# Windowed attention and an MLP mixer on one core: engine order fixed by hand throughout, token weights over SyncE's queue

## The chip, the cores and the metric

The kernel runs on one core of a Trainium2 chip. The metric is device microseconds (us) of one execution; smaller is better. A core has five engines with queues of their own: TensorE (PE; its weight loads are listed as PEld), VectorE (DVE), ScalarE (ACT), GpSimd (POOL) and SyncE (SP). An engine works through its queue in order and waits at an instruction whose inputs or buffers are not free yet.

## The reference

Inputs are q, k, v of shape (8 batches, 8 heads, 576 positions, 64), token-mixing weights (576 x 256 and 256 x 576) and channel-mixing weights (512 x 1536 and 1536 x 512), all float32. With x the attention output laid out as (batch, 576, 512):

```
scores = q @ k.T / 8, less slope(head) * |distance|; only 0 <= distance < 128 counts
x = softmax(scores) @ v
u = x + (relu(x.T @ w_tok1) @ w_tok2).T          # mixes the 576 positions
out = u + relu(u @ w_ch1) @ w_ch2                # mixes the 512 channels
```

## The kernel before

**Tiling.** 576 positions are four blocks of 128 and a rest of 64. Batches go in pairs: a pair has nine blocks, 0 to 3 of its first batch, 4 to 7 of its second, and block 8 (`TAIL`), which holds both rests. The first batch of a pair (half 0) does attention for blocks 0 to 3 and TAIL, the second (half 1) for 4 to 7. Since the window is 128, a block needs its own keys and those of the block before; blocks 0 and 4 need only their own.

**Attention of a block** (`attention`, lines 266 to 300). q and k come in bfloat16 over POOL's queue (`load`, line 95), which converts them on the way; PE transposes them into one PSUM tile `tp` (line 193; eight transposes, four for q and four for k) and VectorE copies that to `qkT` (line 286; line 429 in the first batch). PE makes the scores (line 215) for the even and the odd heads (e = 0, 1) into two PSUM tiles `sp`, one buffer each; ScalarE takes the exponential (line 228) into `pe`; VectorE multiplies by a mask (line 235, `weigh`) that holds the window and the decay with distance; PE multiplies by v (line 253, `values`) into `ot`, whose 65th column is the sum of weights; VectorE normalises (`normalise`: reciprocal, line 259, and product, line 261) into `xb`. Values of one block are emitted after the scores of the next (`held`).

**Token mixing** (`token_mix`): `t1` (line 316) with a relu on ScalarE (line 318) into r1; then for each block `ht` (line 334), to which VectorE adds x (line 335) to give `ub`, and then, after all of these, four transposes of ub (line 340), copied to `uT` (line 346).

**Channel mixing** (`channel_mix`): 12 tiles `ct` of four 512-column matmuls each (line 360), each with a relu on ScalarE (line 362) into r2; in half 1 also three groups `cx` of 16 matmuls of 128 columns for TAIL (line 369). Then, for each of four blocks (five in half 1), 12 matmuls into `o2` (line 378), an add on VectorE (line 382) and the output DMA on SP's queue (lines 385 and 387).

**PSUM.** `tp`, `ot` and `ut` share the pool ps_o with one buffer; `t1`, `ht`, `ct`, `cx` and `o2` share ps_m with three.

**What sets the order.** POOL's queue has the order of the program for the whole kernel (`manual_schedule`). The first batch's attention and token mixing (`first_batch`) are in a second such block, which also fixes PE, ScalarE and VectorE among its own instructions. All that follows on these three engines is put in order by the framework's scheduler, from a cost model of its own and the order of the program; it may set later work between the first batch's instructions. The program mixes batch b's channel mixing with the attention and token mixing of batch b + 1 (`side`) by estimated costs, the numbers after `yield` in ns: `interleave` advances the side until it has done a share (0.78; 1.2 for batch 0, after a lead of 7000 ns) of what the channel mixing has.

**The start.** POOL issues 20 loads of q, k and v for the first batch, then six of the token weights (lines 158 to 166; W1, W2 and their rests, converted to bfloat16 on the way), then the four quarters of the first channel weights (line 173), then blocks 4 to 6 and the four quarters of the second channel weights (line 177). In `first_batch` VectorE also makes masks for TAIL (`make_tail_mask`, lines 141 to 144) in the first two blocks' iterations, and both q and k copies (`settle`). At the end come ht, accumulated on x with the identity (line 494) and W2 (line 503), casts to ub (line 508, on ScalarE and VectorE in turn), and the transposes and copies to uT (lines 452 and 453, `turn_u`), one block behind.

Of the kernel before, what the change touches and what calls it, by code (L numbers as in the profile page):

```python
# [16 lines left out]
def kernel(  # L17
# [47 lines left out]
    ps_m = ctx.enter_context(tc.tile_pool(name="ps_m", bufs=3, space=PS))  # L65

# [90 lines left out]
    def load_token_weights():  # L157
        nc.gpsimd.dma_start(
            out=W1[:, 0:NC, :], in_=moe_w_tok1[0 : NC * P, :].rearrange("(c p) n -> p c n", p=P)
        )  # L160
        w2 = moe_w_tok2.rearrange("(j p) s -> p j s", p=P)
        for i in range(2):
            nc.gpsimd.dma_start(out=W1[i * R : (i + 1) * R, NC + i, :], in_=moe_w_tok1[NC * P : S, :])
        nc.gpsimd.dma_start(out=W2[:, :, :], in_=w2[:, :, 0 : NC * P])
        for i in range(2):
            nc.gpsimd.dma_start(out=W2t[:, i, :, i * R : (i + 1) * R], in_=w2[:, :, NC * P : S])

# [98 lines left out]
    def attention(b):  # L266
# [38 lines left out]
    def token_mix(b):  # L305
# [6 lines left out]
        for j in range(NJ):  # L312
# [5 lines left out]
            nc.scalar.activation(out=r1[:, j, :], in_=t1[:, :], func=ACT.Relu)  # L318
            yield 1080
        r1s[pr, half] = r1  # L320
        uT = rpool.tile([P, NCB, NC * P], BF16, name="uT", tag="uT")
        uTt = None
        if half:
            blocks.append(TAIL)
            uTt = rpool.tile([P, NCB, P], BF16, name="uTt", tag="uTt")
        for blk in blocks:
            ht = ps_m.tile([P, DM], F32, name="ht", tag="m")
            if blk == TAIL:
                mms = [(W2t[:, i, j, :], r1s[pr, i][:, j, :]) for i in range(2) for j in range(NJ)]
            else:  # L330
                c = blk % NC
                mms = [(W2[:, j, c * P : (c + 1) * P], r1[:, j, :]) for j in range(NJ)]
            for n, (l, r) in enumerate(mms):
                nc.tensor.matmul(ht[:, :], lhsT=l, rhs=r, start=n == 0, stop=n == len(mms) - 1)  # L334
            nc.vector.tensor_tensor(out=us[pr][:, blk, :], in0=ht[:, :], in1=xb[:, blk, :], op=ALU.add)  # L335
            yield 432
        for blk in blocks:
            ut = ps_o.tile([P, NCB, P], BF16, name="ut", tag="o")
            for cb in range(NCB):
                nc.tensor.transpose(ut[:, cb, :], us[pr][:, blk, cb * P : (cb + 1) * P], ident[:, :])  # L340
            if blk == TAIL:
                to = uTt[:, :, :]
            else:
                c = blk % NC
                to = uT[:, :, c * P : (c + 1) * P]
            nc.vector.tensor_copy(out=to, in_=ut[:, :, :])
            yield 225
        uts[b] = (uT, uTt)


    def channel_mix(b):
# [5 lines left out]
        for t in range(NHT):  # L357
# [4 lines left out]
            nc.scalar.activation(out=r2[:, t, :], in_=ct[:, :], func=ACT.Relu)  # L362
            yield 864
            if half and t % 4 == 3:
# [6 lines left out]
                nc.scalar.activation(out=r2t[:, t - 3 : t + 1, :], in_=cx[:, :, :], func=ACT.Relu)  # L371
                yield 900
        blocks = list(range(half * NC, (half + 1) * NC)) + ([TAIL] if half else [])
        for blk in blocks:
            o2 = ps_m.tile([P, DM], F32, name="o2", tag="m")
            for t in range(NHT):
                l = r2t[:, t, :] if blk == TAIL else r2[:, t, (blk % NC) * P : (blk % NC + 1) * P]
                nc.tensor.matmul(o2[:, :], lhsT=l, rhs=WC2[:, t, :], start=t == 0, stop=t == NHT - 1)  # L378
                if t % 3 == 2 and t < NHT - 1:
                    yield 648  # L380
            ob = opool.tile([P, DM], F32, name="ob", tag="ob")
# [4 lines left out]
            else:  # L386
                nc.sync.dma_start(out=out[b, (blk % NC) * P : (blk % NC + 1) * P, :], in_=ob[:, :])
            yield 648

# [15 lines left out]

# [6 lines left out]
    def first_batch():  # L412
# [41 lines left out]

        make_masks()
        turn(0)
        settle(0, "q")
        settle(0, "k")
        held = None
        for n, u in enumerate(units):  # L460
# [3 lines left out]
            pe = [exponentials(u, 0, sp[0])]  # L464
            scores(0, u, sp, (1,))
            for blk in nxt:
                turn(blk)
                settle(blk, "q")
                settle(blk, "k")
            pe.append(exponentials(u, 1, sp[1]))  # L470
            if held is not None:
# [5 lines left out]
            else:  # L477
# [84 lines left out]
```

## Time and profile before

| | us |
|---|---|
| median of 3 runs (334.94 to 336.82) | 335.84 |
| the profiled execution, its own time | 334.79 |
| its span, first to last instruction | 333.0 |

| engine | busy us | share of the span | instructions |
|---|---|---|---|
| PE | 306.8 | 92% | 2692 |
| PEld | 165.1 | 50% | 2692 |
| DVE | 169.9 | 51% | 389 |
| ACT | 136.9 | 41% | 208 |
| POOL | 112.1 | 34% | 143 |

The profile has a page (busy time, slices of the span, DMA queues, the chain of work that ended last, the costliest groups of instructions, DMA issues), and the trace under it can be asked for a timeline, for waits, and for busy time by stage. In a line like `x8 [0.30 <-DVE xb L261]` eight instructions are merged, and the engine was idle 0.30 us before them until VectorE had written xb at line 261. In lines by stage the numbers after the stretch are its length, the busy time of PE, PEld, DVE, ACT and POOL with their counts, the granted PE clock, the DMA share and GB/s. A PE line's duration includes the way out of the array, so the next line can start before it ends.

### The profile page before, as it was taken

The page shows a single profiled execution, that of the slowest core. Times are in us where ns is not written, and L with a number is a line of the kernel's source. Part 1 is how long each engine was busy: PE and PEld are TensorE (multiplying, and loading weights), DVE is VectorE, ACT ScalarE, POOL GpSimd, SP SyncE. Part 2 cuts the span into 40 slices and gives each one's busy share as a digit, 9 for nine tenths or more (in the row PEclk, how much of TensorE's full clock was granted, in tenths as well). Part 3 has the DMA queues.
Part 4 walks back from the last instruction along what each step waited for, and adds up shares of the span by engine and source line. Part 5 has one row for each costly group of instructions (what it writes and reads, how often), then busy time and mean ns, then how long its engine had stood idle before and what let it go on. Part 6 is the DMA issues. An engine that isn't in the chain of part 4 may idle for free.

```text
span 333.0 us, 6446 instructions
## 1 busy us (share of the span) xinstructions
PE 306.8 (92%) x2692; PEld 165.1 (50%) x2692; DVE 169.9 (51%) x389; ACT 136.9 (41%) x208; POOL 112.1 (34%) x143
## 2 busy tenths in 40 slices
PE   1787699689999999999999999999999999999993
PEld 1573345335655555455564555455654555455541
DVE  2594306755665646464656547474756447461021
ACT  4451266312864037503863047404772057404600
POOL 8997777799874020523654000000000000000000
PEclk9999699979999999999999999999999999999999
DMA  8999999999999161594999220011000220011022
GB/s 54 145 135 173 162 197 160 179 126 166 171 105 102 65 113 15 35 137 85 107 85 80 94 65 2 1 63 66 2 2 21 75 63 2 0 65 63 2 78 81
DMA packets 123005, 27.81 MB, mean 84 GB/s; under 512 B 113888, under 2 KB 118368, under 8 KB 122976
## 3 DMA queue, kind: packets, MB, share of 16 engines
q0 software_dynamic: 117728, 17.97, 75.4%
q1 hardware_dynamic: 5248, 9.44, 8.3%
q8 instruction: 21, 0.34, 0.4%
q14 instruction: 8, 0.07, 0.1%
HBM read 35.91 MB, written 9.44 MB: 136 GB/s over the span
## 4 chain that ended last, share of the span: by engine, by line
PE 81%; POOL 5%; DVE 5%; DMA 5%; issue 2%; ACT 1%; POOLq 0%
PE o L378 28%; PE ct L360 24%; PE sp L215 5%; PE tp L193 5%; PE ot L253 5%; PE t L316 5%; PE ht L334 4%; DMA kld<-in_k_dram 3%; PE cx L369 3%; PE ut L340 2%; DMA v<-in_v_dram 2%; DVE pe L235 2%; DVE xb L261 2%; POOL kld L95 2%; POOL qld L95 1%
## 5 line engine op out<-in xcount | busy, mean ns | idle before, releaser
L362 ACT ACTIVATE r<-ct 128x512 bf16<-128x512 f32 x96 | 56.2, 601 | 123.4 <-PE ct L360 123.4
L360 PE MATMUL ct<-uT,WC 128*128 128x512 bf16 x384 | 98.3, 384 | 0.1
L378 PE MATMUL o<-WC,r 128*128 128x512 bf16 x384 | 96.4, 379 | 0.5
L228 ACT ACTIVATE pe<-sp 128x1024 bf16<-128x1024 f32 (+1 forms) x72 | 63.0, 927 | 22.5 <-PE sp L215 22.5
L378 PEld LDWEIGHTS <-r 128*128 128x128 bf16 x384 | 35.7, 98 | 36.8 <-issue 2.5
L360 PEld LDWEIGHTS <-WC 128*128 128x128 bf16 x384 | 34.2, 99 | 30.5 <-issue 2.1
L382 DVE TENSOR_TENSOR ob<-o,ub 128x512 f32<-128x512 f32 x36 | 24.7, 687 | 46.2 <-PE o L378 46.2
L235 DVE TENSOR_TENSOR pe<-pe,mask 128x1024 bf16<-128x1024 bf16 (+1 forms) x64 | 39.0, 618 | 17.9 <-ACT pe L228 17.2
L95 POOL DMA_DIRECT2D qld<-in_q_dram x40 | 34.8, 873 | 33.9 <-PE tp L193 29.9
L95 POOL DMA_DIRECT2D v<-in_v_dram x40 | 34.6, 875 | 27.1 <-PE ot L253 13.9
L95 POOL DMA_DIRECT2D kld<-in_k_dram x40 | 34.6, 869 | 5.0 <-DMA WC<-in_moe_w_ch_dram 2.1
L335 DVE TENSOR_TENSOR ub<-ht,xb 128x512 bf16<-128x512 f32 x32 | 21.4, 687 | 23.5 <-PE ht L334 22.9
L253 PE MATMUL ot<-v,pe 128*128 128x65 bf16 (+1 forms) x544 | 29.6, 199 | 3.5 <-DVE xb L261 3.3
L253 PEld LDWEIGHTS <-pe 128*128 128x128 bf16 (+1 forms) x544 | 22.3, 102 | 21.2 <-DVE xb L261 16.4
L286 DVE COPY qkT<-tp 128x1024 bf16<-128x1024 bf16 (+1 forms) x31 | 21.2, 683 | 21.9 <-PE tp L193 21.9
L261 DVE TENSOR_TENSOR xb<-ot,rt 128x256 bf16<-128x256 f32 x72 | 30.5, 424 | 2.4
L215 PE MATMUL sp<-qkT 64*128 64x128 bf16 (+1 forms) x544 | 25.7, 225 | 3.1 <-DVE qkT L429 3.0
L215 PEld LDWEIGHTS <-qkT 64*128 64x128 bf16 x544 | 18.6, 99 | 16.8 <-DVE qkT L286 11.6
L259 DVE RECIPROCAL rt<-ot 128x4 f32<-128x4 f32 x72 | 12.8, 178 | 24.1 <-PE ot L253 23.7
L193 PE MATMUL tp<-ident,qld 128*128 128x128 bf16 x144 | 15.3, 234 | 8.5 <-DMA qld<-in_q_dram 7.5
L316 PE MATMUL t<-xb,W 128*128 128x512 bf16 x70 | 20.2, 393 | 0.7 <-DVE xb L261 0.7
L193 PEld LDWEIGHTS <-qld 128*128 128x128 bf16 x144 | 10.0, 103 | 17.1 <-DMA qld<-in_q_dram 7.9
(58 smaller groups left out, 198.4 us busy)
## 6 DMA issues: line engine op xcount, KB each, us to landing
out_dram<-ob SPq DMA_DIRECT2D x32, 256.0 KB, 2.0
qld<-in_q_dram POOLq DMA_DIRECT2D x32, 128.0 KB, 5.6
kld<-in_k_dram POOLq DMA_DIRECT2D x32, 128.0 KB, 5.3
v<-in_v_dram POOLq DMA_DIRECT2D x32, 128.0 KB, 6.1
WC<-in_moe_w_ch_dram POOLq DMA_DIRECT2D x8, 384.0 KB, 8.4
out_dram<-ob SPq DMA_DIRECT2D x8, 128.0 KB, 2.3
qld<-in_q_dram POOLq DMA_DIRECT2D x8, 64.0 KB, 5.1
kld<-in_k_dram POOLq DMA_DIRECT2D x8, 64.0 KB, 4.3
```

The source lines that it names most:

```text
L95: nc.gpsimd.dma_start(out=got[x][p0 : p0 + n, :, 0:D], in_=rows(SRC[x], b, s0, n))
L193: nc.tensor.transpose(tp[:, "qk".index(x) * NHP + hp, :], loaded[pr, blk][x][:, 2 * hp : 2 * hp + 2, :].rearrange("p h d -> p (h d)"), ide ...
L215: nc.tensor.matmul(sp[e][:, i, kind, c0:c1], lhsT=qkT[pr, kb][e * D : (e + 1) * D, NHP + i, :], rhs=me[e * D : (e + 1) * D, i, c0:c1], sta ...
L228: nc.scalar.activation(out=pe[:, :, f:, :], in_=sp[:, :, f:, :], func=ACT.Exp, scale=scale)
L235: nc.vector.tensor_tensor(out=pe[:, :, f:, :], in0=pe[:, :, f:, :], in1=mk[:, :, f:, :], op=ALU.mult)
L253: nc.tensor.matmul(ot[to, i, :], lhsT=l, rhs=r, start=m == 0, stop=m == len(mms) - 1, skip_group_check=True)
L261: nc.vector.tensor_tensor(out=x4[:, :, e, :], in0=ot[:, :, 0:D], in1=rt[:, :, :].broadcast_to([P, 4, D]), op=ALU.mult)
L316: nc.tensor.matmul(t1[:, :], lhsT=W1[:, c, j * P : (j + 1) * P], rhs=xb[:, blk, :], start=n == 0, stop=n == len(ks) - 1)
L360: nc.tensor.matmul(ct[:, :], lhsT=WC1[:, cb, t * P : (t + 1) * P], rhs=uT[:, cb, :], start=cb == 0, stop=cb == NCB - 1)
L362: nc.scalar.activation(out=r2[:, t, :], in_=ct[:, :], func=ACT.Relu)
L378: nc.tensor.matmul(o2[:, :], lhsT=l, rhs=WC2[:, t, :], start=t == 0, stop=t == NHT - 1)
L382: nc.vector.tensor_tensor(out=ob[:, :], in0=o2[:, :], in1=ub[:, blk, :], op=ALU.add)
```

## The change

- `attention`, `token_mix` and `channel_mix` move into the block that fixes PE, ScalarE and VectorE, so that these three keep the program's order for the whole kernel.
- `interleave` goes. `alternate` advances the side by one step after a step of channel mixing; a side step says by the number that it yields after how many steps the next one comes (1 or 2; 1 at most in batch 0, where five steps of channel mixing run first).
- In `attention` weighing half 1 moves to the start of the next unit's step, and weighing half 0 behind the normalising of half 1 of the unit before. Values of halves 0 and 1 are separate steps, as before.
- In `token_mix` the transposes of a block's u come with the next block's ht instead of after all of them.
- Token weights come as float32 over SP's queue (four DMAs, issued first) into a staging tile in a buffer of r2, and VectorE rounds them to bfloat16 in two groups of copies, one before the first unit and one within it. Both tail masks are made before the first unit.
- In `first_batch` ScalarE instead of VectorE copies q of every block but the first. The exponential of half 1 of the first unit comes before the copies.
- PE gets matmuls of ones with ones into an unused PSUM tile `idle`, which takes a ps_m buffer: 9 at the start, 2 after the first transposes, 8 after the first scores, 3 at the end of each of four units.

The diff, shortened:

```diff
     ps_m = ctx.enter_context(tc.tile_pool(name="ps_m", bufs=3, space=PS))
+    ones = const.tile([P, DM], BF16, name="ones")
+    nc.vector.memset(ones, 1.0)
...
     def load_token_weights():
+        stage = rpool.tile([P, (NC + 1) * DTOK + NJ * S], F32, name="stage", tag="r2")
+        s1 = stage[:, 0 : (NC + 1) * DTOK].rearrange("p (c n) -> p c n", n=DTOK)
+        s2 = stage[:, (NC + 1) * DTOK :].rearrange("p (j s) -> p j s", s=S)
+        nc.sync.dma_start(
+            out=s1[:, 0:NC, :], in_=moe_w_tok1[0 : NC * P, :].rearrange("(c p) n -> p c n", p=P)
         )
         for i in range(2):
+            nc.sync.dma_start(out=s1[i * R : (i + 1) * R, NC, :], in_=moe_w_tok1[NC * P : S, :])
+        nc.sync.dma_start(out=s2[:, :, :], in_=moe_w_tok2.rearrange("(j p) s -> p j s", p=P))
+        return s1, s2
+
+    def round_token_weights(s1, s2, which):
+        copy = nc.vector.tensor_copy
+        if which == 0:
+            copy(out=W1[:, 0:NC, :], in_=s1[:, 0:NC, :])
+            for i in range(2):
+                rs = slice(i * R, (i + 1) * R)
+                copy(out=W1[rs, NC + i, :], in_=s1[rs, NC, :])
+        else:
+            copy(out=W2[:, :, :], in_=s2[:, :, 0 : NC * P])
+            for i in range(2):
+                copy(out=W2t[:, i, :, i * R : (i + 1) * R], in_=s2[:, :, NC * P : S])
...
     def attention(b):
...
-                yield 450
+                yield 1
             got = None
+            if held is not None:
+                weigh(held[0], 1, held[1][1])
             if u is not None:
                 sp = [score_tile(e) for e in range(2)]
                 scores(pr, u, sp, (0, 1))
                 got = (u, [exponentials(u, e, sp[e]) for e in range(2)])
-                for e in range(2):
-                    weigh(u, e, got[1][e])
-                yield 700
-            if held is not None:
-                for e in range(2):
+            for e in range(2):
+                if held is not None:
                     normalise(pr, held[0], e, values(pr, held[0], e, held[1][e], ps_o, "o"))
-                    yield 300
+                if got is not None and e:
+                    weigh(u, 0, got[1][0])
+                yield 1
             held = got
...
     def token_mix(b):
...
-            yield 1080
+            yield 1 + (j == NJ - 1)
...
-        for blk in blocks:
+        for n, blk in enumerate(blocks + [None]):
...
+            if n:
+                last = blocks[n - 1]
+                ut = ps_o.tile([P, NCB, P], BF16, name="ut", tag="o")
...
+            yield 2
...
-    def interleave(main, other, share, lead):
-        done_m, done_o = -float(lead), 0.0
-        for cost in main:
-            done_m += cost
-            while done_o < done_m * share:
-                c = next(other, None)
-                if c is None:
-                    break
-                done_o += c
+    def alternate(main, other, lead, most):
+        for _ in main:
+            lead -= 1
+            if lead < 0:
+                lead = min(next(other, 1), most) - 1
...
     def first_batch():
...
+        idle = ps_m.tile([P, DM], F32, name="idle", tag="m")
+
+        def keep_busy(n):
+            for _ in range(n):
+                nc.tensor.matmul(idle[:, :], lhsT=ones[:, 0:P], rhs=ones[:, :], start=True, stop=True)
+
+        keep_busy(9)
...
             to = qk_tile(0, blk)
-            nc.vector.tensor_copy(out=to[:, sl, :], in_=tp[:, sl, :])
+            if x == "q" and blk:
+                nc.scalar.copy(out=to[:, sl, :], in_=tp[:, sl, :])
+            else:
+                nc.vector.tensor_copy(out=to[:, sl, :], in_=tp[:, sl, :])
...
         turn(0)
+        keep_busy(2)
         settle(0, "q")
         settle(0, "k")
+        round_token_weights(*staged, 0)
+        for e in range(2):
+            make_tail_mask(e)
...
             scores(0, u, sp, (1,))
+            if n == 0:
+                keep_busy(8)
+                pe.append(exponentials(u, 1, sp[1]))
             for blk in nxt:
                 turn(blk)
                 settle(blk, "q")
                 settle(blk, "k")
-            pe.append(exponentials(u, 1, sp[1]))
+            if n:
+                pe.append(exponentials(u, 1, sp[1]))
...
-                if n < 2:
-                    make_tail_mask(n)
+                if n == 0:
+                    round_token_weights(*staged, 1)
             held = (u, pe)
+            if u != TAIL:
+                keep_busy(3)
...
         with tc.manual_schedule(engines={ET.PE, ET.Activation, ET.DVE}):
+            staged = load_token_weights()
             first_loads()
-            load_token_weights()
...
             first_batch()
-        other = side(1)
-        for b in range(B):
-            interleave(channel_mix(b), other, *((1.2, 7000) if b == 0 else (0.78, 0)))
+            other = side(1)
+            alternate(channel_mix(0), other, 5, 1)
             drain(other)
-            other = side(b + 2)
+            for b in range(1, B):
+                other = side(b + 1)
+                alternate(channel_mix(b), other, 0, 2)
+                drain(other)
```

More of the change, by code (lines that the diff above doesn't have):

```diff
@@ L157, in load_token_weights @@
     def load_token_weights():
-        nc.gpsimd.dma_start(
-            out=W1[:, 0:NC, :], in_=moe_w_tok1[0 : NC * P, :].rearrange("(c p) n -> p c n", p=P)
+        stage = rpool.tile([P, (NC + 1) * DTOK + NJ * S], F32, name="stage", tag="r2")
[3 more added lines that the diff above has]
+            out=s1[:, 0:NC, :], in_=moe_w_tok1[0 : NC * P, :].rearrange("(c p) n -> p c n", p=P)
         )
-        w2 = moe_w_tok2.rearrange("(j p) s -> p j s", p=P)
         for i in range(2):
[L163 to L166, printed above, removed]
+            nc.sync.dma_start(out=s1[i * R : (i + 1) * R, NC, :], in_=moe_w_tok1[NC * P : S, :])
[12 more added lines that the diff above has]
+                copy(out=W2t[:, i, :, i * R : (i + 1) * R], in_=s2[:, :, NC * P : S])
     def load_channel_weights(which, x):
@@ L325, in token_mix @@
             uTt = rpool.tile([P, NCB, P], BF16, name="uTt", tag="uTt")
-        for blk in blocks:
[L327 to L347, printed above, removed]
+        for n, blk in enumerate(blocks + [None]):
+            if blk is not None:
+                ht = ps_m.tile([P, DM], F32, name="ht", tag="m")
+                if blk == TAIL:
+                    mms = [(W2t[:, i, j, :], r1s[pr, i][:, j, :]) for i in range(2)
+                           for j in range(NJ)]
+                else:
+                    c = blk % NC
+                    mms = [(W2[:, j, c * P : (c + 1) * P], r1[:, j, :]) for j in range(NJ)]
+                for m, (l, r) in enumerate(mms):
+                    nc.tensor.matmul(ht[:, :], lhsT=l, rhs=r, start=m == 0, stop=m == len(mms) - 1)
+                nc.vector.tensor_tensor(out=us[pr][:, blk, :], in0=ht[:, :], in1=xb[:, blk, :],
+                                        op=ALU.add)
+            if n:
+                last = blocks[n - 1]
+                ut = ps_o.tile([P, NCB, P], BF16, name="ut", tag="o")
+                for cb in range(NCB):
+                    nc.tensor.transpose(ut[:, cb, :], us[pr][:, last, cb * P : (cb + 1) * P],
+                                        ident[:, :])
+                if last == TAIL:
+                    to = uTt[:, :, :]
+                else:
+                    c = last % NC
+                    to = uT[:, :, c * P : (c + 1) * P]
+                nc.vector.tensor_copy(out=to, in_=ut[:, :, :])
+            yield 2
@@ L362, in channel_mix @@
             nc.scalar.activation(out=r2[:, t, :], in_=ct[:, :], func=ACT.Relu)
-            yield 864
+            yield
             if half and t % 4 == 3:
@@ L371, in channel_mix @@
                 nc.scalar.activation(out=r2t[:, t - 3 : t + 1, :], in_=cx[:, :, :], func=ACT.Relu)
-                yield 900
+                yield
         blocks = list(range(half * NC, (half + 1) * NC)) + ([TAIL] if half else [])
@@ L379, in channel_mix @@
                 if t % 3 == 2 and t < NHT - 1:
-                    yield 648
+                    yield
             ob = opool.tile([P, DM], F32, name="ob", tag="ob")
@@ L387, in channel_mix @@
                 nc.sync.dma_start(out=out[b, (blk % NC) * P : (blk % NC + 1) * P, :], in_=ob[:, :])
-            yield 648
+            yield
     def drain(g):
@@ L428, in settle @@
             to = qk_tile(0, blk)
-            nc.vector.tensor_copy(out=to[:, sl, :], in_=tp[:, sl, :])
+            if x == "q" and blk:
+                nc.scalar.copy(out=to[:, sl, :], in_=tp[:, sl, :])
+            else:
+                nc.vector.tensor_copy(out=to[:, sl, :], in_=tp[:, sl, :])
         def average(blk, e, pe):
```

## The prediction

> **What bounds the kernel now.** I read the page's slices first, then the busy time by stage, then the chain that ended last, then the timeline. The slices (PE, POOL and granted clock in tenths, 40 slices of 8.3 us):
>
> ```profile
> PE   1787699689999999999999999999999999999993
> POOL 8997777799874020523654000000000000000000
> PEclk9999699979999999999999999999999999999999
> ```
>
> PE is full from slice 11 on; holes are in the first nine slices and the last. Stages are cut at the first channel-mix matmul of each batch, which the chain gives (columns: start us, us, what):
>
> ```profile
> 39.95 9.47 PE ct L360 x36
> ...
> 79.34 0.86 PE ct L360 x4
> ...
> 120.13 0.86 PE ct L360 x4
> ...
> 153.56 0.86 PE ct L360 x4
> ...
> 301.97 3.45 PE ct L360 x16
> 305.42 0.89 PE cx L369 x16
> ...
> 315.01 12.96 PE o L378 x60
> ```
>
> So: 39.95 us before channel mixing starts, 39.4 for batch 0, then 40.8 and 33.4 in turn, and 31.0 for batch 7, which has nothing beside it. Batch 7 is PE work without a gap (3.45 is 16 x 0.216). Busy time by stage (length, PE, PEld, DVE, ACT, POOL, clock):
>
> ```profile
> 39.95:79.34 39.39, 35.98 (x264) 16.94 (x265) 18.03 (x40) 15.07 (x22) 31.81 (x39) 0.92 1.99 164
> 79.34:120.13 40.79, 40.34 (x400) 22.25 (x398) 23.15 (x49) 17.98 (x27) 20.68 (x25) 1.00 1.41 120
> 120.13:153.56 33.43, 33.21 (x276) 17.05 (x274) 18.97 (x41) 14.46 (x22) 7.87 (x9) 1.00 0.66 68
> ```
>
> Batches 1 to 6 leave PE idle 0.2 to 0.45 us each. Counting each matmul at its back-to-back spacing (0.216 for 512 columns, 0.056 for a transpose, 0.03 to 0.04 for a value product), 1.4 and 0.7 us are unfilled. Six such batches hold 6.3 us at most, so **a new order can win little there and lose much**; what can be won lies in the first two stages, 79.3 us long.
>
> **The start.** PE runs at half speed at first: transposes stand 0.106 us apart up to 21.8 us and 0.056 at 33 us, so the 9s of PEclk there are not to be believed. In windows of 4 us the granted clock is 0.53 from 36 to 40 us, and the first 12 ct matmuls stand 0.427 apart instead of 0.216: 2.5 us. The end of the start (start us, us, then the idle time before in brackets):
>
> ```profile
> 34.39 0.42 DVE L453 COPY uT<-ut 128x512 bf16<-128x512 bf16 x1 [0.49 <-PE ut L452]
> ...
> 36.90 0.61 PE L193 MATMUL tp<-ident,qld 128*128 128x128 bf16 x4 [2.55 <-DMA qld<-in_q_dram]
> ...
> 38.28 1.06 PE L452 MATMUL ut<-ident,ub 128*128 128x128 bf16 x8
> ```
>
> Batch 1's transposes stand in PE's queue ahead of batch 0's last two u transposes and wait for q. Fixed order puts those first: ScalarE ends block 2's cast at 34.75, its transposes and copy take 1.1; VectorE ends block 3's cast at 35.47, transposes at 35.5, copy to 36.4, ct at 36.5. That is 3.5 us, without any other edit.
>
> VectorE paces the five units before. **Token weights off POOL**: six issues, 4.9 us between the first of them (19.09) and the first channel weights (23.98), so these and batch 1's q are issued 4.9 earlier; q at about 32 instead of 36.9 waits for no one. SP's four transfers run beside the first q and k: nothing, if they fit in the idle first 4 us, to 3.2 us (640 KB of rounded weights at the 198 GB/s of 28 to 32 us); I take 0.7, as 0 to 4 us move only 24 GB/s. SP's queue holds nothing else before the first output at 59 us. **Rounding**, float32 in SBUF, has no row: a 1024-column copy lies between 0.27 (the 512-column bfloat16 mask copy) and 1.4 (twice the 0.69 cast of 512 columns from PSUM). Nearest is the mask copy, whose two instances took 0.27 and 0.83 with POOL issuing; I take 0.9, and 0.25 for each of the two small pieces: 1.4 a half. It waits for SP's transfers, and behind it in VectorE's queue stand the tail masks and block 1's k, for which scores 1 wait. Four q copies of 0.41 go to ScalarE, which has room (1.94 + 0.58 in a unit of about 3).
>
> Hand-walk of VectorE: first copies end at 8.5 (7.83 + 0.7), rounding to 9.9, both tail masks (2.4, moved here from units 0 and 1) to 12.3, block 1's k to 12.7, scores 1 at 12.8 against 11.5. Then weighing (0.7) and rounding (1.4) to 14.8; units 1 and 2 at 0.34 + 2.3 each, to about 20.2; the TAIL transposes lack a ps_m buffer, which `idle` holds, and come at 20.4; scores of TAIL 21.5 against 22.6; block 3 normalised at 24.6, t1 at 24.65 against 26.59. From there the chain is the old one: ct at 36.5 - 1.9 = 34.6. If PE is still cold when the eight dummies run (8 x 0.427 = 3.4), block 1's copy slips from 12.3 to 13.7: ct at 35.9. I take 35.2: **-4.7 us**. The 31 dummies are 6.7 us of PE at 0.216; a unit's three stand beside VectorE's 2.9 (transposes 0.45, scores 0.56, values 0.5 and dummies 0.65 are 2.2), and without that cover they cost what sticks out, 1.5 a unit at twice the spacing (4.4 against 2.9). Between the last token product and ct, PE has 16 transposes in 3.2 us, as before, when the clock fell after the like; 0.7 us for that risk is charged to batch 0.
>
> In this trace the spacing halves only between 21.8 and 24.9 us, after ten busy microseconds with gaps. The Trainium skill ("TensorE: Matmul & The Clock Gate", Part 1) has the clock rise after about 3.4 us of sustained work; by that, nine dummies would barely suffice and ct would come at 34.6, where the trace's slower rise would give 35.9. A row for the rounding's other victim is the mask copy, 0.27 and 0.83 beside POOL's issues. The skill's "SBUF — State Buffer" ("SBUF: two separate sides") speaks against the change here: a float32 VectorE copy within SBUF holds a port pair that POOL needs to write descriptors. By that rule POOL's loads would lose the copies' time as well, and the sum would be up to 2.8 us worse.
>
> **Batch 0's channel mixing.** Its PE work by spacing is 32.6: 20.7 for its own steps (3 x 3.45 and four fifths of 12.96, from batch 7) and 11.9 for the side. Five steps run alone, then one side step after each. From the scores of block 6 on attention lies beside output products of 3 x 0.216 = 0.65 instead of 0.86, and there VectorE sets the pace; by the walk below the waits are 0.28 before, then 0.31, 0.25, 0.25, 0.09, 0.56, 0.87 and 0.25: 2.9. With 0.5 in token mixing, 0.5 at the end and 0.7 for the clock 37.2 against 39.4: **-2.2**.
>
> **Batches 1 to 6.** Delays from the timeline of batch 2 (score products, then values of half 0, normalising, values of half 1):
>
> ```profile
> 130.19 0.41 PE L253 MATMUL ot<-v,pe 128*128 128x65 bf16 x8
> ...
> 130.65 0.18 DVE L259 RECIPROCAL rt<-ot 128x4 f32<-128x4 f32 x1 [1.07 <-PE ot L253]
> 130.86 0.42 DVE L261 TENSOR_TENSOR xb<-ot,rt 128x256 bf16<-128x256 f32 x1
> 131.34 0.42 PE L253 MATMUL ot<-v,pe 128*128 128x65 bf16 x8
> 131.35 0.69 DVE L235 TENSOR_TENSOR pe<-pe,mask 128x1024 bf16<-128x1024 bf16 x1
> ```
>
> The values take 0.25 to issue, VectorE starts 0.21 later, 0.63 on it is done, 0.06 later PE may use the one ps_o buffer again: 0.90 between two uses. A ct step of 0.86 covers all but 0.04, an output step of 0.65 all but 0.25. A unit with its transposes, in the new order: copy at 0, scores 0.76 to 1.32, values 0 to 1.57, ct, values 1 at 2.47 to 2.72, ct, transposes 3.62 to 4.07, copy at 4.27 (VectorE, with weighing half 0 behind the second normalising, is free at 4.09), scores due at 4.93, possible at 5.03. Waits 0.18 a unit; the old order has the same. The **last unit** differs: no transposes follow, and weighing half 0 is queued behind normalising half 1 of the unit before. In an even batch: values 1 of unit 6 issued by 5.64, normalised at 6.48, weighed 6.40 to 7.09, values of unit 7 at 7.16 where PE is free at 6.50: 0.66 lost, then 0.25 at the next. In an odd batch these steps lie beside output products: 0.25 + 0.87 + 0.30. In all 1.5 and 2.25 us, against 0.7 and 1.4: **3 x 0.8 + 3 x 0.9 = +5.1**. Token mixing two steps apart (1.3 us) covers relu (0.87) and the add (0.95), so it costs nothing; one step apart in batch 0 it is charged above. Batch 7 keeps its 31.0.
>
> **Sum**: -4.7 - 2.2 + 5.1 = -1.8. Span 333.0 becomes 331.2, with the 1.8 around it (334.8 for 333.0) 333.0; the median of the runs, 335.8, is 1.0 above the profiled execution, so 334.0.
>
> **Rivals.** (1) *The lockstep costs nothing more* than the old order: then -6.9, 328.9. For it: waits of 0.04 and 0.1 stand in both orders. Against: the last unit's queue order is fixed. (2) *Slower: VectorE's queue becomes the loop in every unit.* Its margin in a unit is 0.18 (free at 4.09, transposes done at 4.27). If weighing starts over 0.18 late, because exponentials stand behind relus on ScalarE (1.94 + 3 x 0.6 of 4.27 us), each of some 27 units loses what is over; at 0.25 a unit that is 6.8, and -1.8 + 6.8 = +5: 341. It decides from 1.2 us more a batch than the old order's waits (6.9 / 6). For it: 88% of ScalarE's time; against: half 0 is ready at 2.44, a full microsecond before its turn. (3) *The start does not move*: SP's transfers take 3.2, dummies run cold, the fall of the clock repeats. Then -1.9 for 4.7, net +1.0 to 337; for it the early contention, against it the 3.5 that the queue order alone gives. An order that is not what the edit says would show at once as batch 1's transposes ahead of u's.
>
> **How the numbers follow.** Forecast 0.50 (of it 0.26 below -0.5%, 0.17 within, 0.07 above, as start and last unit each have some 2 us of doubt); rival 1 0.18, faster; rival 2 0.22, slower; rival 3 0.10, half same, half slower. About 0.5%, 1.7 us, is what a measurement can tell from no change. Faster 0.44, same 0.22, slower 0.34. The forecast's own range is 330 to 338; to hold 8 in 10 it must reach rival 1 and most of rival 2: 328 to 341.5.
>
> **What would show it.** ct starts at 34.6 to 36 with 0.216 spacing; transposes before 20 us 0.056 apart; batch 0 about 37; odd and even batches about 41.7 and 34.2, with values L253 waiting for pe L235 once a batch for over half a microsecond. Even batches at or under 33.4 would be rival 1; PE waiting at scores for qkT in every unit would be rival 2; ct at 38 or later rival 3.

## The result, and the profile after

The changed kernel takes 330.84 us, median of its runs, against 335.5 before; the ratio is 0.9854, 95% interval 0.9816 to 0.9892: **faster by 1.5%**. The forecast was 334.0 (328 to 341.5), so the time lies in its range and its sign is right, and yet two of its three terms are wrong by 4 to 5 us and cancel. One execution ran at a mean granted clock of 0.566 (520.94 us) and is left out; as it was the profiled one, the profile read here is of the same kernel run again (331.18, ratio 0.9851; profiled execution 330.56, span 328.8).

Slices of the changed kernel (8.2 us each), PE, POOL and clock:

```profile
PE   4887699899989999999999999999999999999994
POOL 8986958899752020705843000000000000000000
PEclk9999999999999999999999999999999999999998
```

PE's first slices are fuller than before (4 instead of 1 in the first, 8 instead of 6 in the eighth), where matmuls of ones count as busy. Busy time by stage, columns as before, cut at the first `ct` matmul of batches 0, 1, 2 and 3:

```profile
39.36:74.89 35.53, 33.36 (x272) 16.63 (x279) 18.59 (x41) 14.78 (x22) 29.77 (x36) 1.00 2.03 170
74.89:115.97 41.08, 39.95 (x393) 22.31 (x398) 23.26 (x49) 18.09 (x27) 20.35 (x25) 1.00 1.45 117
115.97:149.19 33.22, 32.27 (x270) 16.46 (x274) 18.89 (x41) 14.36 (x22) 7.86 (x9) 1.00 0.67 68
```

Batch 0 shrinks to 35.53 and its clock goes from 0.92 to 1.00. (From one first `ct` matmul to the next it was 39.23 before; the 39.39 shown there ended at a later one of these matmuls. All stages from here on are cut at the first.) Odd batches grow from 40.79 to 41.08 and even ones shrink from 33.42 to 33.22. The end of the start, in the timeline (start us, us, what, idle time before):

```profile
36.08 0.39 PE L480 MATMUL ut<-ident,ub 128*128 128x128 bf16 x4
36.78 0.40 PE L480 MATMUL ut<-ident,ub 128*128 128x128 bf16 x4 [0.32 <-DVE ub L546]
37.63 0.40 PE L480 MATMUL ut<-ident,ub 128*128 128x128 bf16 x4 [0.45 <-ACT ub L546]
38.35 0.40 PE L480 MATMUL ut<-ident,ub 128*128 128x128 bf16 x4 [0.33 <-DVE ub L546]
39.36 1.89 PE L381 MATMUL ct<-uT,WC 128*128 128x512 bf16 x7 [0.61 <-DVE uT L481]
```

No transposes of batch 1 stand among them any more, and PE waits only for the casts and copies of u: the order is what the edit says. But this stretch begins 2.8 us later than before (36.08 against 33.26), which eats nearly all of what the order wins.

| stage (us) | before | forecast | changed |
|---|---|---|---|
| start, to the first `ct` matmul | 39.95 | 35.2 (-4.7) | 39.36 (-0.6) |
| batch 0 | 39.23 | -2.2 | 35.53 (-3.7) |
| batches 1 to 6 | 3 x 40.79 + 3 x 33.42 | +5.1 | 3 x 41.08 + 3 x 33.22 (+0.3) |
| batch 7 | 31.22 | 0 | 31.00 (-0.2) |
| span | 333.0 | 331.2 (-1.8) | 328.8 (-4.2) |

### The profile page after: what moved, and what is told of

Read it like the earlier page. It is cut to its first block, busy times and chain, and to the rows that moved or that the text cites. A ratio compares the mean times of both kernels' runs of the same rounds, so it can differ in the third digit from the quotient of the medians.

```text
span 519.1 us, 6511 instructions
## 1 busy us (share of the span) xinstructions
PE 505.5 (97%) x2723; PEld 228.7 (44%) x2723; DVE 173.5 (33%) x392; ACT 143.4 (28%) x212; POOL 108.6 (21%) x137
## 4 chain that ended last, share of the span: by engine, by line
PE 91%; DMA 5%; POOL 2%; DVE 1%; issue 1%; ACT 0%; POOLq 0%
PE o L399 31%; PE ct L381 28%; PE ht L353 5%; PE t L333 5%; PE tp L209 5%; PE ot L269 5%; PE sp L231 4%; PE cx L390 4%; DMA WC<-in_moe_w_ch_dram 4%; PE ut L360 2%; DMA kld<-in_k_dram 1%; PE idle L440 1%; DVE pe L251 1%; POOL v L97 0%; POOL WC L189 0%
## 5 line engine op out<-in xcount | busy, mean ns | idle before, releaser
L399 PE MATMUL o<-WC,r 128*128 128x512 bf16 x384 | 162.1, 580 | 0.0
L381 PE MATMUL ct<-uT,WC 128*128 128x512 bf16 x384 | 160.5, 578 | 0.6 <-DMA WC<-in_moe_w_ch_dram 0.6
L399 PEld LDWEIGHTS <-r 128*128 128x128 bf16 x384 | 46.8, 130 | 67.0 <-issue 66.4
L381 PEld LDWEIGHTS <-WC 128*128 128x128 bf16 x384 | 46.6, 131 | 63.0 <-issue 61.9
L269 PEld LDWEIGHTS <-pe 128*128 128x128 bf16 (+1 forms) x544 | 28.8, 110 | 28.1 <-DVE xb L277 10.0
L269 PE MATMUL ot<-v,pe 128*128 128x65 bf16 (+1 forms) x544 | 36.2, 221 | 0.6
L231 PE MATMUL sp<-qkT 64*128 64x128 bf16 (+1 forms) x544 | 29.6, 262 | 0.0
L333 PE MATMUL t<-xb,W 128*128 128x512 bf16 x70 | 29.6, 581 | 0.0
L353 PE MATMUL ht<-r,W 128*128 128x512 bf16 x56 | 27.1, 578 | 0.0
L335 ACT ACTIVATE r<-t 128x512 bf16<-128x512 f32 x14 | 8.4, 597 | 57.0 <-PE t L333 57.0
```

What stands on the lines that cost most here:

```text
L231: nc.tensor.matmul(sp[e][:, i, kind, c0:c1], lhsT=qkT[pr, kb][e * D : (e + 1) * D, NHP + i, :], rhs=me[e * D : (e + 1) * D, i, c0:c1], sta ...
L269: nc.tensor.matmul(ot[to, i, :], lhsT=l, rhs=r, start=m == 0, stop=m == len(mms) - 1, skip_group_check=True)
L333: nc.tensor.matmul(t1[:, :], lhsT=W1[:, c, j * P : (j + 1) * P], rhs=xb[:, blk, :], start=n == 0, stop=n == len(ks) - 1)
L353: nc.tensor.matmul(ht[:, :], lhsT=l, rhs=r, start=m == 0, stop=m == len(mms) - 1)
L381: nc.tensor.matmul(ct[:, :], lhsT=WC1[:, cb, t * P : (t + 1) * P], rhs=uT[:, cb, :], start=cb == 0, stop=cb == NCB - 1)
```

## The experiments

Each kernel was timed in three rounds beside the kernel before; ratios are to that, with 95% intervals. Stages are those of its profiled execution (us).

| kernel | time | ratio | first `ct` | batch 0 | odd, even |
|---|---|---|---|---|---|
| e1 changed, again | 331.18 | 0.9851 (0.9812 to 0.9889) | 39.36 | 35.53 | 41.08, 33.22 |
| e2 order alone | 328.09 | 0.9762 (0.9719 to 0.9804) | 36.77 | 35.53 | 41.07, 33.22 |
| e3 start alone | 334.02 | 0.9936 (0.9911 to 0.9961) | 39.93 | 38.88 | 40.79, 33.42 |
| e4 changed, no dummies | 332.62 | 0.9885 (0.9841 to 0.9928) | 40.43 | 37.21 | 41.07, 33.23 |
| e5 e2 + SyncE's loads, unread | 329.98 | 0.9831 (0.9809 to 0.9853) | 38.45 | 35.53 | 41.07, 33.22 |
| e6 changed, weights over POOL | 328.46 | 0.9789 (0.9774 to 0.9804) | 36.62 | 35.53 | 41.08, 33.22 |
| e7 e2 + last unit reordered | 324.46 | 0.9684 (0.9652 to 0.9716) | 36.63 | 34.92 | 40.63, 32.77 |
| e8 e6 + last unit reordered | 323.99 | 0.9663 (0.9634 to 0.9693) | 35.11 | 35.89 | 40.62, 32.78 |
| e9 changed, one load held | 329.33 | 0.9805 (0.9786 to 0.9823) | 38.79 | 35.52 | 41.07, 33.22 |
| e10 changed, no rounding | 331.0 | 0.9854 (0.9835 to 0.9873) | 39.24 | 35.53 | 41.07, 33.22 |
| e11 e2 + dummies | 327.72 | 0.9753 (0.9731 to 0.9774) | 35.81 | 36.31 | 41.07, 33.22 |
| e12 e10, eight dummies less | 329.38 | 0.9803 (0.9769 to 0.9837) | 38.07 | 35.54 | 41.07, 33.23 |

In e1 to e4 the theory is the prediction's; from e5 on a theory is what the runs before it suggested. The rival is the other account that the run is to tell it from.

### The parts apart (e1 to e4)

e1 is the changed kernel, no edit.

> The changed kernel again, for a profile at the full clock. Theory (as predicted): the start and batch 0 give 6.9 us and batches 1 to 6 give part of it back, so channel mixing starts at 34.6 to 36 us, batch 0 takes about 37, and the batches in turn take about 41.7 and 34.2 against 40.8 and 33.4, each with one wait of values (L253) for the weighing over half a microsecond. Rival: the fixed order costs nothing in batches 1 to 6 (40.8 and 33.4 or less), and the start moved by less than 3 us. Time 330.8 either way.

The start moved by 0.6, as the rival had it, and the batches are the old sum, as the rival had it; but the wait that the theory named is there once a batch (below).

e2 is the kernel before with the order alone: one block that fixes the order, `alternate`, the new steps of `attention` and `token_mix`. The first batch is the old one, with token weights over POOL and no dummies.

> The kernel before with only the fixed order and the one-step-at-a-time interleaving; its first batch and token weights are as before (POOL's queue, no dummies, no rounding). Theory: the u transposes come ahead of batch 1's, so channel mixing starts near 36.5 instead of 39.95, still at half clock at first; batch 0 about 37 to 39; batches 1 to 6 lose 5: in all within 1.5 us of the kernel before, 334 to 337. Rival (the order wins in the batches, the first-batch edits nothing): 331, as fast as the changed kernel.

It goes further than the rival: **the order alone beats the whole change by 3 us.** Its `ct` starts at 36.77, where the forecast's walk from the old timeline had 36.5.

e3 is the reverse: the edits of the first batch, with the old `interleave` and the framework's order after it.

> The changed kernel with only the first-batch edits (token weights on SP, rounding, dummies, copies on ScalarE); the scheduler orders the rest and may again set batch 1's transposes early. Theory: channel mixing starts at 35 to 37, batches 1 to 6 keep 40.8 and 33.4: 329 to 332. Rival (the order is what gains): 334 or more.

334.02 is the rival's side. `ct` does not move (39.93), scores of unit 1 come at 16.42 instead of 11.49.

e4 is the changed kernel without the 31 matmuls of ones and their buffer.

```diff
-            for _ in range(n):
+            for _ in range(0):
-        idle = ps_m.tile([P, DM], F32, name="idle", tag="m")
```

> The changed kernel without the matmuls of ones and without the buffer that they hold. Theory: PE stays at half clock to some 20 us and falls again before channel mixing; ct about 1 us later and its first 12 to 16 matmuls 0.427 apart: 2 to 4 us slower than the changed kernel, 333 to 335. Rival (VectorE paces the start whatever PE's clock is): 330.8, within 0.5.

The median is 1.4 above e1's, the intervals overlap, with runs from 330.73 to 333.4, so the time alone does not settle it. The profiled execution, the slowest of the four, shows a price: `ct` 1.07 later, a granted clock of 0.57 from 40 to 44 us with seven of the first 16 `ct` matmuls at 0.427 us, and a batch 0 longer by 1.68. There the dummies were missed; that all executions without them pay this is not shown (one took 330.73, and e2, without them, has batch 0 at 35.53).

### What holds the start back (e5, e6, e9, e10, e12)

e5 is e2 with SyncE's four loads (`load_unused`) issued first into a tile that nobody reads; the weights that are used come over POOL.

```diff
+            load_unused()
             first_loads()
```

> The fixed order alone (328.1 us), with SP's four float32 loads of the token weights added at the start into a tile that nothing reads; the weights in use still come over POOL. Theory: the loads alone hold up the first q and k, whose transposes move from 4.9 and 6.2 to near 8.8 and 9.7 us as in the changed kernel; channel mixing starts 2 to 4 us later than 36.8: 330 to 332 us. Rival (VectorE's rounding and moved masks are what costs, the loads fit beside the others): q's transposes stay near 5 us, 328 to 328.5.

The theory's side: q comes 4 us later and the time is 329.98, its lower edge, though `ct` moves by 1.7 only (38.45 against 36.77) and not by 2 to 4. First the stretch from 2 to 4 us in e5, then in e2, then PE's first work in e2 and in e5 (the last two columns of a stretch are DMA share and GB/s):

```profile
2.00:4.00 2.00, 0.00 (x0) 0.00 (x0) 0.00 (x0) 0.02 (x1) 1.93 (x5) 1.00 0.91 290
```

```profile
2.00:4.00 2.00, 0.00 (x0) 0.00 (x0) 0.00 (x0) 0.03 (x1) 1.93 (x5) 1.00 0.72 46
```

```profile
4.94 0.61 PE L193 MATMUL tp<-ident,qld 128*128 128x128 bf16 x4 [4.94 <-DMA qld<-in_q_dram]
```

```profile
8.96 0.61 PE L204 MATMUL tp<-ident,qld 128*128 128x128 bf16 x4 [8.96 <-DMA qld<-in_q_dram]
```

q's 128 KB, issued at 1.25 in both, land 4.0 us later, when nearly all of SyncE's 1216 KB have landed (the last 576 KB, issued at 2.49, take 6.6 us). The idle DMA engines of the first 4 us, on which the forecast's 0.7 rested, took up only part of the loads: by 4 us 0.59 of SyncE's 1.25 MB had moved. The rest moved side by side with q and slowed it: from 4 to 6 us the engines moved 740 packets of POOL's queue (0.09 MB) and 126 of SyncE's (0.19 MB), where in e2 POOL's queue alone moved 1502 packets (0.19 MB) from 3 to 5 us.

e6 is the changed kernel with the token weights back on POOL and no rounding; dummies, moved masks and ScalarE's copies stay.

```diff
-            staged = load_token_weights()
             first_loads()
+            load_token_weights()
```

> The changed kernel with the token weights back on POOL's queue after the first loads, converted on the way, no staging and no rounding; dummies, q copies on ScalarE, early tail masks and fixed order stay. Theory (the loads over SP cost the start): q's transposes near 5 us, PE at full clock earlier than with the order alone, channel mixing starts at 35 to 36.8: 326 to 328 us. Rival (dummies and moved copies cost as well): 329 or more.

`ct` at 36.62 is the theory's 35 to 36.8, the time of 328.46 just above its bound: without SyncE's loads the rest of the start's edits costs nothing in time, and wins nothing either. Its `ct` is one profile's: e8, below, has the same start and `ct` at 35.11. In e6 PE is at half speed again at 21.53, where three dummies take 1.47 us, and 0.81 in e8.

e9 holds the first of SyncE's loads, 512 KB, behind a write of POOL into its tile; it is issued at 4.71 instead of 0.74, the other three (704 KB) still at 0.7 to 2. (The call moves into `first_loads`.)

```diff
+        nc.gpsimd.memset(stage[:, 0:1], 0.0)
```

> The changed kernel with SP's first transfer held until GpSimd, after issuing the first q and k, has written one column of the staging tile (near 4.7 us). Theory (the transfers cost because they are ahead of the first q and k): q's and k's transposes return to about 5 and 6.3 us; the transfers now hold up block 1's q and k, for which VectorE's rounding and masks leave some room; channel mixing starts at 37 to 38.5 instead of 39.4, 328.5 to 330 us. Rival (1.2 MB ahead of the later blocks costs the same wherever it stands): 39 to 40, 330.5 or more.

The time, 329.33, is the theory's; `ct`, at 38.79, falls between the two. q comes back to 7.21 only. Block 1's q and k, issued at 4.66 and 5.57, take 5.9 and 5.8 us and so are there by 11.4, but PE is at its eight dummies until 13.42, at half speed for most of them:

```profile
10.04 3.59 PE L444 MATMUL idle<-ones 128*128 128x512 bf16 x8
13.42 0.51 PE L213 MATMUL tp<-ident,qld 128*128 128x128 bf16 x4
```

Beside e5 this gives the measure of the delay: 704 KB cost q 2.27 us (7.21 against 4.94) and 1216 KB 4.0, both 310 to 320 GB/s, although the 576 KB among them are issued after q (0.7 us in e9, 1.2 in e5).

e10 is the changed kernel without rounding: SyncE's transfers land unread, POOL loads the weights.

```diff
-        round_token_weights(*staged, 0)
...
-                    round_token_weights(*staged, 1)
```

> The changed kernel with SP's loads as they are, into the staging tile, but read by nothing; the weights in use come over POOL, so VectorE rounds nothing. Theory (rounding, 3.4 us of VectorE in the changed kernel's profile, stands in the chain of the start): q's transposes stay near 8.8, channel mixing starts at 37 to 38.4 instead of 39.4, about 1 to 2 us less. Rival (the rounding is hidden behind the late loads): 39 to 39.5, 330.5 to 331.

The rival: 39.24 and 331.0, where the kernel with its rounding has 39.36 and 331.18. So rounding is hidden, though its copies take 1.12, 0.69, 0.95 and 0.65, 3.4 in all instead of the estimated 2.8. What stays between e10 (39.24) and e5 (38.45) is not rounding. In e10's timeline q and k of block 1 have landed, and PE is still at its dummies:

```profile
11.50 2.66 PE L437 MATMUL idle<-ones 128*128 128x512 bf16 x8
...
13.99 0.39 PE L206 MATMUL tp<-ident,qld 128*128 128x128 bf16 x4
...
15.26 0.42 DVE L454 COPY qkT<-tp 128x512 bf16<-128x512 bf16 x1 [2.56 <-ACT qkT L452]
```

VectorE has done its masks and waits 2.56 us for a copy of q on ScalarE, which waits for these transposes. Either the eight dummies or the move of q's copy could be the cause. e12 takes the eight out of e10:

```diff
-                keep_busy(8)
```

> This is the run without rounding (SyncE's transfers land in a tile that nobody reads, GpSimd loads the weights), now also without the eight matmuls of ones that stand in TensorE's queue ahead of block 1's transposes; the other 23 stay. Theory (the eight dummies are the rest of the start's delay): block 1's transposes stand at 11.5 to 12 us instead of 13.99, scores of unit 1 at about 13.8 instead of 15.74, and channel mixing starts at 38.3 to 38.7, where the run with the order alone and the same idle transfers had 38.45; the time is 330.2. Rival (ScalarE's copies of q, for which VectorE's copy of k waits in every unit, are the rest): the scores of unit 1 move in the same way, but the later units wait as before, channel mixing starts at 39.0 to 39.4, and the time is 331.0. Should the clock rise later for want of the eight, transposes still stand 0.106 apart after 15 us and channel mixing starts after 39.4.

The theory's side: transposes at 11.99, scores of unit 1 at 14.23, `ct` at 38.07, 1.17 earlier and below the 38.3 that the theory had at best. As it is 0.4 below e5, ScalarE's copies, the early masks and the other 23 dummies cost nothing together; one by one they are not told apart. The time is 329.38; ratio 0.9803 against 0.9854, with intervals that just overlap and runs that do not.

### The dummies with early loads (e11)

e2 with the 31 dummies and nothing else of the new start.

> The fixed order alone (328.1 us) with the 31 matmuls of ones added and nothing else. Theory (VectorE paces the first units, PE reaches full clock by itself before channel mixing): within 0.7 us of the order alone, 327.4 to 328.8, though transposes stand 0.056 apart sooner. Rival (PE's half clock costs the start): channel mixing starts at 34.5 to 35.8 instead of 36.8, 326 to 327.2.

As the theory has it, nothing that the time can tell (327.72 and 328.09), though `ct`, 0.96 earlier, is at the rival's edge: batch 0 is 0.78 longer. What is gained is taken back at the output products of batch 0, where PE now waits for the second channel weights, and did not in e2:

```profile
53.94 0.81 PE L385 MATMUL o<-WC,r 128*128 128x512 bf16 x3 [0.62 <-DMA WC<-in_moe_w_ch_dram]
```

e8, with `ct` at 35.11, waits there for 0.79. In these two runs an earlier start runs into POOL's weight loads; e2 and e7 (`ct` at 36.77 and 36.63) do not wait there. The clock, in e11, rises within the first nine dummies; the line after e11's two is e1's:

```profile
1.46 3.49 PE L425 MATMUL idle<-ones 128*128 128x512 bf16 x9 [1.46 <-DVE v L74]
5.09 0.40 PE L195 MATMUL tp<-ident,qld 128*128 128x128 bf16 x4
```

```profile
1.46 4.02 PE L440 MATMUL idle<-ones 128*128 128x512 bf16 x9 [1.46 <-DVE v L74]
```

In e11 transposes at 5 us stand 0.056 apart, not 0.106 (0.61 for four). In e1 all of the nine stand 0.427 apart, so the clock is not up when they end; PE then waits 3.35 us for q, and the transposes after it take 0.61. e6, with early loads, has the same 4.02 for nine, and its first transposes, with no wait before them, are at half speed too (0.63). So the first nine do not always bring the clock up.

### The last unit (e7, e8)

The forecast's loss in batches 1 to 6 was that weighing half 0 of the last unit is queued on VectorE behind normalising half 1 of the unit before, though no transposes follow that need that order. e7 is e2 with weighing half 0 first in that case alone (`wait` is true where transposes follow); e8 is the same edit on e6.

```diff
+                if got is not None and e and not wait:
+                    weigh(u, 0, got[1][0])
                 if held is not None:
...
-                if got is not None and e:
+                if got is not None and e and wait:
```

> The fixed order alone (328.1 us) with one edit in attention: where no transposes are left, weighing half 0 goes ahead of normalising half 1 of the unit before. Theory: the wait of 0.64 us of values for the weighing in each even batch, and of about 0.9 in each odd one, goes: even batches from 33.2 to 32.5 to 32.8, odd ones from 41.1 to 40.1 to 40.5, in all 3 to 6 us less, 322 to 325. Rival (the wait turns into one of values of half 1 for the ps_o buffer, as VectorE has the same work in front of it): 327.5 to 328.5.

> Both: token weights on POOL in the changed kernel, and the edit of the last unit. Theory: the two gains add, as they are in different stages: e6's time less 3 to 6 us, 321 to 324. Rival: as e6.

Both times as expected, 324.46 and 323.99: 0.44 to 0.45 off every odd and even batch and 0.61 off batch 0, 3.4 us of span for e7 (326.4 to 323.0). Odd batches stay a little above the 40.1 to 40.5 expected. **e8 takes 323.99, ratio 0.9663 (0.9634 to 0.9693), faster than both kernels.** Its interval overlaps e7's, so beside the order and this one move, the other edits of the start show no gain in time. The place in batch 2, first in the changed kernel:

```profile
131.13 0.42 DVE L277 TENSOR_TENSOR xb<-ot,rt 128x256 bf16<-128x256 f32 x1
131.22 1.15 ACT L383 ACTIVATE r<-ct 128x512 bf16<-128x512 f32 x2
131.47 1.28 DVE L251 TENSOR_TENSOR pe<-pe,mask 128x1024 bf16<-128x1024 bf16 x2
132.21 0.42 PE L269 MATMUL ot<-v,pe 128*128 128x65 bf16 x8 [0.47 <-DVE pe L251]
```

PE's four `ct` matmuls at 130.71 end at 131.74, and PE is idle for 0.47 us until the first of the two weighings is through. In e7 half 0 is weighed before the normalising, and the values follow with no idle time shown before them:

```profile
126.68 0.69 DVE L235 TENSOR_TENSOR pe<-pe,mask 128x1024 bf16<-128x1024 bf16 x1
...
127.98 0.41 PE L253 MATMUL ot<-v,pe 128*128 128x65 bf16 x8
```

Of all waits of PE in the execution, this group's in the changed kernel (total us, times, longest), and what is left for values in e7:

```profile
PE ot L269 <- DVE pe L251: 4.3, 8, 0.7
```

```profile
PE ot L253 <- DVE xb L261: 1.1, 4, 0.4
```

## Why the prediction was right in sum and wrong in its terms

**The start (-4.7 forecast, -0.6 measured).** The order's part stands: 3.5 walked, 3.18 measured (e2). The step that failed is the part that the other edits were to add, -1.2 forecast, **+2.6** measured. By differences of the runs' first `ct`: SyncE's loads +1.68 (e5 less e2), the eight dummies +1.17 (e10 less e12), ScalarE's copies of q and the other edits -0.38 (e12 less e5), rounding +0.12 (e1 less e10); with -3.18 these make -0.59. (These are differences of single profiles. e6 and e8, with the same start, are 1.5 apart, so the two small ones cannot be told from nothing; the median times go with the two large ones, 1.9 for e5 less e2 and 1.6 for e10 less e12.)

- *SyncE's loads.* The term was 0.7 at q, with bounds of 0 and 3.2; measured 4.0 at q, outside the bounds, of which 1.7 reach `ct`. Two mistakes: the bound took 640 KB, the size after rounding, where 1216 KB of float32 travel, and the 0.7 took the idle time of the first 4 us for room enough, where less than half of the bytes had moved by then and the rest slowed q. The walk had VectorE's first copies end at 8.5; they end at 11.1.
- *The eight dummies.* The forecast charged them only if PE were cold, and by a copy at 13.7 instead of 12.3. PE was cold: in e1 the first nine dummies all ran at half speed, and PE then had nothing to do for 3.35 us, as q came late. The eight, about half of them cold (2.54 us), then stood in PE's queue ahead of transposes whose data were there. With early loads the eight take 1.90 and show no price (e6, e11).
- *Rounding* was in the walk's chain at 1.4 a half. It is on no chain: without it, PE is what VectorE waits for. The Trainium skill ("SBUF — State Buffer", the box on VectorE blocking DMA) says that such float32 copies keep GpSimd from writing descriptors. By that rule e10 should gain some of the copies' 3.4 us (POOL has six issues more there, but later than the first loads); e1 and e10 differ by 0.12 at `ct` and 0.2 in time, so nothing of it reaches the end here.
- For the start rival 3 is the nearest to what came: it had SyncE's transfers as its mechanism, left -1.9, and its sign, `ct` at 38 or later, showed.

**Batch 0 (-2.2 forecast, -3.7 measured).** Right in sign. 37.2 was walked, 35.53 measured: the 0.7 set aside for the clock was not needed (1.00), and the side's PE work, put at 11.9, is some 11.2 by the spacing that its products have where nothing holds them; that leaves 3.6 of waits where 3.9 were walked. By start-to-start times PE spends 2.0 on the value products instead of 4.8, 10.7 instead of 12.1 on `ct` and 2.2 instead of 3.5 on `t1`, but 13.2 instead of 11.5 on `o2`; the wait of values for `xb` was 2.5 in this stage before and is 0.4. e2 and e1 have the same 35.53, and e3, with the old order, 38.88, so it is the order that brings it, and not the dummies. (The forecast read the first 12 `ct` matmuls of the kernel before at half speed, 2.5 us; eight were, some 1.6.)

**Batches 1 to 6 (+5.1 forecast, +0.3 measured).** The walk of the new order is nearly right: over back-to-back spacing batch 2 loses 1.5 (1.5 walked; 1.25 at `ct`, of it 0.47 of idle, and 0.24 at `o2`) and batch 1 2.0 (2.25 walked), and e7 takes 0.45 a batch away by the one edit that the walk points to. The step that failed is the price of the **old** order's waits, put at 0.7 for an even and 1.4 for an odd batch: by the same count they are 1.7 in both. Lines of the kernel before, in batch 2, show what was missed:

```profile
129.64 0.62 PE L215 MATMUL sp<-qkT 64*128 64x128 bf16 x16
...
130.29 1.94 ACT L228 ACTIVATE pe<-sp 128x1024 bf16<-128x1024 f32 x2 [0.60 <-PE sp L215]
...
131.70 1.19 PE L215 MATMUL sp<-qkT 64*128 64x128 bf16 x16
...
132.28 0.43 PEld L215 LDWEIGHTS <-qkT 64*128 64x128 bf16 x8 [0.20 <-issue]
```

The same 16 score products take 0.57 longer the second time: ScalarE's two exponentials of the unit before, which empty the two `sp` tiles with one buffer each, end at 132.23, and the weights of the second eight are loaded from 132.28 on. This wait lies within a line that the trace merges and counts as busy. Sums of start-to-start times in batch 2 show it too: score products 2.56 before and 1.99 after, `t1` 2.51 and 2.16, `ct` 10.96 and 11.62, and all together 33.42 and 33.22. So the old order lost 0.9 in scores and `t1` alone, where 0.7 had been counted for all. The forecast's 11.9 for the side is 0.9 above the 11.0 of such sums over all the side's products without waits, as if scores and `t1` had been taken with their waits for work. The lockstep loses as much elsewhere, and rival 1 (it costs nothing more) was right for these batches, not for its reason. Rival 2 did not come: no wait at scores for `qkT` after the start.

**Sum.** 4.1 too good at the start, 1.5, 4.8 and 0.2 too bad behind it: span 331.2 forecast, 328.8 measured. The time was right in its range by cancelling.

Not tried: the change with its token weights over SyncE's queue behind the first q and k altogether; e9 held one load of four.

## What to carry to other kernels

Time the old order's waits in the same way as the new order's, from start to start and within merged lines, or the difference is mostly the one that was counted less. A load that is moved to another queue to free its issuer still shares the DMA engines: price it in bytes as they leave memory; issued within a microsecond or so of what the first engine waited for, it cost the time of all of them here, and part of that reached the end of the start. When a fixed order shows one recurring wait, look for the step whose reason for standing there does not hold (here the last unit), and move that one: it won 3.4 us of span, where the whole change won 4.2.

## What the runs showed of the hardware that had not been expected

- Loads over SyncE's queue hold back a smaller load over GpSimd's by about their bytes at 310 to 320 GB/s: q's 128 KB by 2.27 us beside 704 KB and by 4.0 beside 1216 KB, with SyncE's loads issued from 0.5 us before q to 1.2 us after it. The Trainium skill ("DMA: Bandwidth & Descriptors", "SWDGE vs HWDGE vs iDMA") says that a DMA engine takes turns between the queues that these two feed. The trace agrees as far as it goes: packets of both queues move in the same stretch (e5, 4 to 6 us), GpSimd's of 128 bytes and SyncE's of 1 to 2.3 KB. What share of the delay comes of the turns no run here separates.
- The time that back-to-back matmuls of ones take to bring the clock up differs between executions: their spacing halves some 2.9 us after the first in e11 and 3.3 us after it in e12 (3.49 and 3.71 for nine), and has not halved in e1 and e6 after 3.8 us (4.02 for nine). In e12 the transposes after 3.14 idle us are at half speed again (0.61 for four). The slow rise that the forecast read from the kernel before (after 21.8 us) fits the gaps in its work; no run here shows that they are its cause. The Trainium skill ("TensorE: Matmul & The Clock Gate", Part 1) gives about 3.4 us for the rise; these rows lie on both sides of it.
